# Two gated linear-attention blocks on one core: B's q by seven products per pair of row blocks, woven with B's k chunks

## The chip, the core and the metric

One core of one Trainium2 chip. The metric is the device time of one execution in microseconds; a kernel's time is the median of its runs. TensorE multiplies into PSUM (eight banks of 512 fp32 columns in each of 128 partitions), VectorE (DVE), ScalarE (ACT) and GpSimd (POOL) do the elementwise work, and SyncE (SP) issues most transfers.

## The reference

The input x has 2048 rows of 640 numbers. Two blocks, A and B, have weights of their own and read the same x. All data are bf16.

```python
def block(x, wqkv, wo):                       # A and B alike
    qkv = (x @ wqkv).reshape(B, S, 3, H, Dh)  # S = 2048, H = 32 heads of Dh = 20
    q, k, v = ...                             # each B, H, S, Dh
    phi = lambda t: jnp.where(t > 0, t + 1, jnp.exp(t)) + 1e-6
    pq, pk = phi(q), phi(k)
    kv  = einsum("bhsd,bhse->bhde", pk, v)
    z   = einsum("bhsd->bhd", pk)
    num = einsum("bhqd,bhde->bhqe", pq, kv)
    den = einsum("bhqd,bhd->bhq", pq, z)[..., None] + 1e-6
    return merge_heads(num / den) @ wo

g = sigmoid((x * gate_w).sum(-1, keepdims=True))
out = g * block(x, A_wqkv, A_wo) + (1 - g) * block(x, B_wqkv, B_wo)
```

## The kernel before

Rows are cut into 16 tiles of 128 (`ST`), features into 5 tiles of 128 (`DT`). `xT` holds x transposed (features on partitions), `xn` holds x with rows on partitions, `pk` holds phi(k) with rows on partitions and `pqT[b]` phi(q) transposed. v is never formed: G = xᵀ·pk is multiplied by wv (`kvt_mm`), masked to the heads' diagonal blocks (`kvt_mask`, into `KVT`), and multiplied by wo into one 640 x 640 matrix `M[b]` (`m_unit`), so that the output is pq·M. The row normalisation and the gate go into pqT (`rec_pass`, `norm_spread`, `scale`). Weights' columns are taken with a step of 5 (`mixed`), and every sum over features and every row tile is a group of matmuls in PSUM.

The order of the work:

1. A's k in 16 chunks (`k_chunk`: ten 128x320 matmuls, L205), with half of A's q between them (`q_block`, `q_unit`: ten 128x512 matmuls, L265 and L254). `phi` follows each: ScalarE takes the exponential (L195), VectorE clamps it (L198) and takes the maximum with the value plus one from PSUM (L202). In the "lifted" form ScalarE also copies the value plus one to SBUF (L197), and VectorE's maximum is a bf16 TensorTensor (L200).
2. The rest of A's q (`q_pass(0, ...)`), with the gate (`gate_pass`) and z (`z_rows`, `z_pass`).
3. A's G (`g_all`): one plain column block (`g_pass`, L288), then `g_strassen`, which computes a 2 x 2 block product by seven products instead of eight (L315). Its bf16 sums are `x_sum` and `k_sum` on VectorE. In its middle stand `rec_pass` (denominators on TensorE, then two steps `d` and two reciprocals on VectorE) and `norm_spread` (exA, L491), which TensorE does between two of the seven products.
4. B's k in 16 chunks, with A's `kvt_pass` after the second and four `p_diff` (sums for the output stage) on VectorE.
5. B's q (`q_pass(1, ...)`): ten units, with z and A's five `m_unit` between them.
6. B's G, as A's.
7. B's M, then the output: eight `Pair`s of row tiles, again seven products for a 2 x 2 block product of [pqA pqB] and [M_A; M_B].

Most of the instruction order is written by hand (`manual_schedule`); each engine runs its queue in order. PSUM in stages 1 to 6 is one pool of four slots of two banks (`ps0` to `ps3`), taken in turn unless a slot is named. A buffer's next user waits for the last reader of the one before. B's weights reuse A's buffers: `wk[1]` is loaded when A's last k chunk is done, `wq[1]` when A's q is done, `wv[1]` behind A's `kvt_pass`, B's wo behind A's last `m_unit`. All four go out on SP's queue, in that order and ahead of the output's stores.

Of the kernel before, what the change touches and what calls it, by code (L numbers as in the profile page):

```python
# [8 lines left out]
P = 128  # L9
# [22 lines left out]
def kernel(  # L32
# [19 lines left out]
    banks = ctx.enter_context(ExitStack())  # L52
    psum = banks.enter_context(tc.tile_pool(name="psum", bufs=1, space=bass.MemoryType.PSUM))

    turn = [0]

    def ps_raw(name, slot=None):

        if slot is None:
            slot = turn[0]  # L60
            turn[0] = (slot + 1) % 4
        return psum.tile([P, 4 * HB], BF16, tag=f"ps{slot}", name=name)
# [18 lines left out]
    R = persist.tile([P, 2, 4, RB], BF16, name="R")  # L81
    ones = persist.tile([P, H], BF16, name="ones")
    gwr = persist.tile([P, DT, H], BF16, name="gwr")
    D3 = persist.tile([P, DT, SH], BF16, name="D3")
# [6 lines left out]
    S3 = persist.tile([P, 3, hc, ic], BF16, name="S3")  # L91
    SX = {k: S3[:, k - 1] for k in (1, 2, 3)}
# [3 lines left out]
    lift = persist.tile([P, 1], FP32, name="lift")  # L96
    TM = [persist.tile([P, DT, HF], BF16, name="TM0")] + [None] * 3
    ge = [persist.tile([P, 2 * RB], FP32, name=f"ge{b}") for b in "AB"]
# [93 lines left out]
    def phi(dst, src, n, lifted=False):  # L192

        e = work.tile([P, 2, n], BF16, tag="e", name="e", bufs=3)
        nc.scalar.activation(out=e[:], in_=src, func=ACT.Exp)  # L195
        if lifted:
            nc.scalar.activation(out=dst, in_=src, func=ACT.Identity, bias=lift[:])  # L197
        nc.vector.tensor_scalar(e[:], e[:], 1.0, EPS, op0=ALU.min, op1=ALU.add)  # L198
        if lifted:
            nc.vector.tensor_tensor(out=dst, in0=dst, in1=e[:], op=ALU.max)  # L200
            return
        nc.vector.scalar_tensor_tensor(out=dst, in0=src, scalar=1.0 + EPS, in1=e[:], op0=ALU.add, op1=ALU.max)  # L202
# [7 lines left out]
    def k_done(b, i, pt):  # L210
        phi(pk[:, i, :].rearrange("p (b n) -> p b n", b=2), pt[:, :, 0:HF], HF)
# [32 lines left out]
    def mixed(t, m):  # L244

        return t[:, m::DT]

    def q_unit(b, m, h, lifted=False):

        pt = ps(f"q{'AB'[b]}")  # L250
        for u in range(2):
            for c in range(DT):
                n = 2 * h + u
                nc.tensor.matmul(  # L254
                    pt[:, u, :], lhsT=mixed(wq[b][:, c, :], m), rhs=xT[:, c, n * HB:(n + 1) * HB],
                    start=(c == 0), stop=(c == DT - 1),
                )
        phi(pqT[b][:, m, h * 2 * HB:(h + 1) * 2 * HB].rearrange("p (b n) -> p b n", b=2), pt, HB, lifted)

    def q_block(b, m, n):  # L260

        pt = ps(f"q{'AB'[b]}")
        for u in range(2):
            for c in range(DT):
                nc.tensor.matmul(  # L265
                    pt[:, u, :], lhsT=mixed(wq[b][:, c, :], m + u), rhs=xT[:, c, n * HB:(n + 1) * HB],
                    start=(c == 0), stop=(c == DT - 1),
                )
        phi(pqT[b][:, m:m + 2, n * HB:(n + 1) * HB], pt, HB)
# [94 lines left out]
    def z_rows(b):  # L364

        pt = ps(f"z{'AB'[b]}")
# [7 lines left out]
        zr = work.tile([P, D], BF16, tag="zr", name="zr")  # L374
# [6 lines left out]
    def z_pass(b, zr):  # L381

        pt = ps(f"zs{'AB'[b]}")
# [8 lines left out]
    def kvt_mm(b, pt, hf):  # L392

        for j in range(4):
            for c in range(DT):
                nc.tensor.matmul(  # L396
                    pt[:KG, hf, j * KG:(j + 1) * KG], lhsT=wv[b][:, c, (4 * hf + j) * KG:(4 * hf + j + 1) * KG],
                    rhs=GT[hf][:, c, j * KG:(j + 1) * KG], start=(c == 0), stop=(c == DT - 1),
                )

    def kvt_mask(pt, hf):

        nc.vector.tensor_tensor(
            out=KVT[:KG, 2 * hf:2 * hf + 2, 0:3:2, :],
            in0=pt[:KG, hf, 0:HF].rearrange("p (g k n) -> p g k n", g=2, k=2),
            in1=maskE[:KG, None, None, :].to_broadcast([KG, 2, 2, KG]), op=ALU.mult,
        )

    def kvt_pass(b):

        pt = ps("kvA")
        for hf in range(2):
            kvt_mm(b, pt, hf)
        for hf in range(2):
            kvt_mask(pt, hf)
# [106 lines left out]
    def tmp(name, tag):  # L522
        return work.tile([P, HF], FP32, tag=tag, name=name)

    class Pair:
# [13 lines left out]
        def p1(self):  # L539
            prod(self.at("x"), pqT[0][:, :, 0:SH], M[0][:, :, 0:HF], self.i, True)  # L540
            self.p1s = work.tile([P, HF], FP32, tag="e", name="p1s", bufs=3)
            nc.scalar.copy(out=self.p1s[:], in_=self.at("x"))
# [12 lines left out]
        def p6(self):  # L555
            prod(self.at("x"), xT[:, :, 0:SH], TM[1], self.i, False)
            self.u2 = tmp("u2", "ex")
            nc.scalar.copy(out=self.u2[:], in_=self.at("x"))  # L558
            self.u3 = tmp("u3", "zr")
            out_add(self.u3[:], self.at("y"), self.u2[:])  # L560
# [39 lines left out]
    def q_pass(b, units):  # L600

        units = list(units)
        q_unit(b, *units.pop(0))
        if b == 0:
            gate_pass()
        zr = z_rows(b)
        if b == 1:
            m_unit(0, 0, "act")
        for k in range(2):
            if b == 0:  # L610
                x_sum(1 + k)
            q_unit(b, *units.pop(0), b == 0)
        zsel = z_pass(b, zr)
        for k, (m, h) in enumerate(units):
            if b == 0 and k < 2:
                if k:
                    x_sum(3)
                else:
                    k_sum(0, 2)
            q_unit(b, m, h, b == 0)  # L620
            if b == 1 and k in (0, 2):
                for c in range(k + 1, k + 3):
                    m_unit(0, c, "act")
            if b == 1 and k == 0:
                k_sum(1, 1)
            if b == 1 and k == 4:
                add_rows(TM[0][:], M[0][:, :, HF:D], M[0][:, :, 0:HF], ALU.subtract)
        if b == 1:
            k_sum(1, 2)
        return zsel  # L630

    def g_all(b, zsel):

        g_pass(b, DT - 1, 1)
        k_sum(b, 3)
        g_strassen(b, zsel)

# [3 lines left out]
    turn[0] = 2  # L641
    for n in range(2):
        for i in range(CB if n else 0, CB * 2 * n):
            k_chunk(0, i)
        for m in (0, 2):
            q_block(0, m, n)
    q_unit(0, DT - 1, 0)
    for i in range(hc, ST - 2):
        k_chunk(0, i)
# [10 lines left out]
    def late_pool(name):  # L660
        return tc.tile_pool(name=name, bufs=1, space=bass.MemoryType.PSUM, reuse_waits="tile")

# [3 lines left out]
    with tc.manual_schedule():  # L666
# [5 lines left out]
        zsel = q_pass(0, [(m, 1) for m in range(DT)])  # L672
# [22 lines left out]
        part = [slice(n * RB, (n + 1) * RB) for n in range(4)]  # L695
# [3 lines left out]
        with late_pool("mid") as mid:  # L699
            first = bank(mid, "mid0", 2)  # L700
            kv = bank(mid, "mid1", 2)
            kvt_mm(1, kv, 0)
            kvt_mask(kv, 0)
            pairs[0].p1()
            kvt_mm(1, kv, 1)
            kvt_mask(kv, 1)
# [89 lines left out]
```

## Time and profile before

| | |
|---|---|
| median of 3 runs | 192.13 us (191.94 to 192.37) |
| the profiled execution | 192.89 us |
| its span, first to last instruction | 191.1 us, TensorE clock 1.000 |
| busy time | PE 185.4, DVE 146.9, ACT 74.0, POOL 8.5 us |
| A's k and first half of q | 7.8 to 41.6 us |
| A's q, rest, and A's G | 39.5 to 74.3 us |
| B's k | 74.3 to 97.5 us |
| B's q | 97.5 to 124.0 us |
| B's G | 124.0 to 145.3 us |
| B's M and the output | 145.3 to 191.1 us |

Times on the page are microseconds from the start of the span unless marked ns. A group's line gives the line of the code, the engine, the operation, output and inputs with their shapes, the count, then busy time and mean ns of one, then the idle time of the engine ahead of them and what ended it. In a timeline the first number is the start and the second the duration; an engine's sign with q (SPq) means its instruction queue, here a transfer's issue. Matmuls overlap: the pace of a run of matmuls is read from their starts. A few matmul records are missing from the trace.

### The profile page before, as it was taken

To read this page: it belongs to the slowest core of one execution; us is meant where nothing else is said; L and a number is where in the kernel's file an instruction comes from. 1 tells how busy PE (TensorE), PEld (TensorE's weight loads), DVE (VectorE), ACT (ScalarE), POOL (GpSimd) and SP (SyncE) were. 2 spreads that over 40 slices of the span, in tenths; PEclk is the share of its full clock that TensorE was granted. 3 is DMA by queue.
4 is the path that set the end of the run, shared out by engine and by line. 5 is a ranking of instruction groups with operands and counts; after the bars stand their busy time and mean duration, and the time that the engine had idled before them with its cause. 6 is when DMAs were issued, how large, how long until landed. Compare 5 with 4: busy or idle time off the path is not lost.

```text
span 191.1 us, 3763 instructions
## 1 busy us (share of the span) xinstructions
PE 185.4 (97%) x1567; PEld 125.1 (65%) x1575; DVE 146.9 (77%) x236; ACT 74.0 (39%) x104; POOL 8.5 (4%) x23
## 2 busy tenths in 40 slices
PE   8799999999999999999999999999999999999993
PEld 3466657765577677877765555577677776777772
DVE  1378968899893997799985785895797989788554
ACT  2055446455942532254544545431621611111120
POOL 8900000000000000000000000000000000000000
PEclk9999999999999999999999999999999999999999
DMA  6976549981050000320000006100000002312222
GB/s 175 328 142 86 106 77 368 301 198 50 2 172 3 0 0 0 67 108 0 3 0 0 3 2 144 31 0 0 3 0 0 3 0 70 125 70 71 74 77 69
DMA packets 18879, 13.99 MB, mean 73 GB/s; under 512 B 9392, under 2 KB 18864, under 8 KB 18864
## 3 DMA queue, kind: packets, MB, share of 16 engines
q1 hardware_dynamic: 18288, 13.11, 26.0%
q10 hardware_dynamic: 576, 0.66, 1.0%
q8 instruction: 12, 0.20, 0.5%
q14 instruction: 3, 0.02, 0.0%
HBM read 9.18 MB, written 2.62 MB: 62 GB/s over the span
## 4 chain that ended last, share of the span: by engine, by line
PE 93%; DMA 3%; DVE 1%; ACTq 0%; issue 0%; ACT 0%; DVEq 0%
PE gs L315 16%; PE qB L254 11%; PE kB L205 11%; PE kA L205 11%; PE qA L254 7%; PE ox L515 6%; PE oy L515 5%; PE oz L515 5%; PE qA L265 4%; DMA xn<-in_A_x_dram 3%; PE ow L515 2%; PE gB L288 2%; PE gA L288 2%; PE mA L429 2%; DVE osb L520 1%; PE mid L396 1%
## 5 line engine op out<-in xcount | busy, mean ns | idle before, releaser
L205 PEld LDWEIGHTS <-xT 128*128 128x128 bf16 x320 | 31.0, 98 | 12.5 <-DVE xT L190 0.5
L198 DVE TENSOR_SCALAR e<-e 128x640 bf16<-128x640 bf16 (+1 forms) x52 | 18.8, 361 | 11.6 <-ACT e L195 11.1
L205 PE MATMUL kA<-wkA,xT 128*128 128x320 bf16 x160 | 22.6, 299 | 0.1
L254 PE MATMUL qB<-xT,wqB 128*128 128x512 bf16 x96 | 22.3, 380 | 0.2
L205 PE MATMUL kB<-wkB,xT 128*128 128x320 bf16 x160 | 22.1, 299 | 0.0
L254 PEld LDWEIGHTS <-wqB 128*128 128x128 bf16 x100 | 11.4, 118 | 9.7 <-issue 0.7
L195 ACT ACTIVATE e<-kB 128x640 bf16<-128x640 f32 x16 | 11.3, 704 | 14.2 <-PE kB L205 12.2
L195 ACT ACTIVATE e<-kA 128x640 bf16<-128x640 f32 x16 | 11.1, 704 | 13.8 <-PE kA L205 13.8
L195 ACT ACTIVATE e<-qB 128x1024 bf16<-128x1024 f32 x10 | 10.2, 1023 | 12.7 <-PE qB L254 12.7
L202 DVE SCALAR_TENSOR_TENSOR pk<-kA,e 128x640 bf16<-128x640 f32 x16 | 13.2, 825 | 1.7
L202 DVE SCALAR_TENSOR_TENSOR pk<-kB,e 128x640 bf16<-128x640 f32 x16 | 13.2, 825 | 1.7
L195 ACT ACTIVATE e<-qA 128x1024 bf16<-128x1024 f32 x10 | 10.2, 1023 | 10.6 <-PE qA L254 5.2
L254 PE MATMUL qA<-xT,wqA 128*128 128x512 bf16 x58 | 13.5, 380 | 0.1
L202 DVE SCALAR_TENSOR_TENSOR pqTB<-qB,e 128x1024 bf16<-128x1024 f32 x10 | 12.3, 1225 | 1.4 <-DVE e L198 0.5
L558 ACT COPY u<-ox 128x320 f32<-128x320 f32 x8 | 3.4, 425 | 21.9 <-PE ox L515 21.9
L315 PEld LDWEIGHTS <-S 128*128 128x128 bf16 x96 | 9.1, 98 | 4.2 <-issue 0.8
L315 PEld LDWEIGHTS <-xn 128*128 128x128 bf16 x96 | 9.4, 98 | 3.6
L254 PEld LDWEIGHTS <-wqA 128*128 128x128 bf16 x60 | 6.9, 118 | 5.6 <-issue 0.3
L515 PEld LDWEIGHTS <-xT 128*128 128x128 bf16 x85 | 8.0, 98 | 3.1 <-DVE xT L454 0.2
L515 PEld LDWEIGHTS <-pqTA 128*128 128x128 bf16 x85 | 7.9, 98 | 2.9 <-issue 0.2
L515 PEld LDWEIGHTS <-pqTB 128*128 128x128 bf16 x80 | 7.8, 98 | 3.0
L315 PE MATMUL gs<-pk,xn 128*128 128x320 bf16 x64 | 9.3, 299 | 0.0
(121 smaller groups left out, 280.4 us busy)
## 6 DMA issues: line engine op xcount, KB each, us to landing
out_dram<-osb SPq DMA_DIRECT2D x14, 160.0 KB, 1.8
xn<-in_A_x_dram SPq DMA_DIRECT2D x3, 640.0 KB, 6.2
wqA<-in_A_wqkv_dram SPq DMA_DIRECT2D x1, 800.0 KB, 6.4
wvA<-in_A_wqkv_dram SPq DMA_DIRECT2D x1, 800.0 KB, 9.9
woA<-in_A_wo_dram SPq DMA_DIRECT2D x1, 800.0 KB, 11.9
wkB<-in_B_wqkv_dram SPq DMA_DIRECT2D x1, 800.0 KB, 4.7
wqB<-in_B_wqkv_dram SPq DMA_DIRECT2D x1, 800.0 KB, 4.6
wvB<-in_B_wqkv_dram SPq DMA_DIRECT2D x1, 800.0 KB, 4.7
```

The lines of the kernel that those rows point to most:

```text
L195: nc.scalar.activation(out=e[:], in_=src, func=ACT.Exp)
L198: nc.vector.tensor_scalar(e[:], e[:], 1.0, EPS, op0=ALU.min, op1=ALU.add)
L202: nc.vector.scalar_tensor_tensor(out=dst, in0=src, scalar=1.0 + EPS, in1=e[:], op0=ALU.add, op1=ALU.max)
L205: nc.tensor.matmul(pt[:, hf, 0:HF], lhsT=xT[:, c, i * P:(i + 1) * P], rhs=wk[b][:, c, hf * HF:(hf + 1) * HF], start=(c == 0), stop=(c == D ...
L254: nc.tensor.matmul(pt[:, u, :], lhsT=mixed(wq[b][:, c, :], m), rhs=xT[:, c, n * HB:(n + 1) * HB], start=(c == 0), stop=(c == DT - 1),)
L265: nc.tensor.matmul(pt[:, u, :], lhsT=mixed(wq[b][:, c, :], m + u), rhs=xT[:, c, n * HB:(n + 1) * HB], start=(c == 0), stop=(c == DT - 1),)
L288: nc.tensor.matmul(pt[:, hf, 0:HF], lhsT=xn[:, i, c * P:(c + 1) * P], rhs=pk[:, i, hf * HF:(hf + 1) * HF], start=(i == 0), stop=(i == ST - 1),
L315: nc.tensor.matmul(pt[:, n, 0:HF], lhsT=left[:, i, n * P:(n + 1) * P], rhs=right[:, i, :], start=(first and i == 0), stop=(i == hc - 1), s ...
L396: nc.tensor.matmul(pt[:KG, hf, j * KG:(j + 1) * KG], lhsT=wv[b][:, c, (4 * hf + j) * KG:(4 * hf + j + 1) * KG], rhs=GT[hf][:, c, j * KG:(j ...
L429: nc.tensor.matmul(dst[32 * g:32 * g + 32, :], lhsT=mixed(heads, c), rhs=wo_sb[b][:KG, 2 * g + k, hf * HF:(hf + 1) * HF], start=(k == 0), ...
L515: nc.tensor.matmul(dst, lhsT=left[:, c, r0:r0 + P], rhs=right[:, c, :], start=(first and c == 0), stop=(c == DT - 1), skip_group_check=not ...
L558: nc.scalar.copy(out=self.u2[:], in_=self.at("x"))
```

## The change

- **Seven products.** For B, the features 0 to 511 of x (two by two tiles), four of the five column tiles of wq and each pair of 512-row blocks form a 2 x 2 block product. `q_strassen` computes it with seven products of two matmuls each instead of eight; the fifth feature tile is added plainly, and the fifth column tile stays plain (`fifth`). Sums of products are made in the PSUM banks: ScalarE seeds one bank with a copy of another, VectorE adds a saved product (`p5`) from one bank into two others.
- **The sums it needs.** `sq_sum` makes four sums of x for each pair of row blocks, on VectorE: for rows 0 to 1023 between the clamp and the top of three q phis of A and behind one k chunk, for rows 1024 to 2047 ahead of A's `g_strassen`. `tq_sums` makes four sums of wqB on POOL, as soon as wqB has landed.
- **The weave.** B's k chunks 0 to 2 and half of the fifth column tile come first, then four calls of `q_strassen`; in each, up to four fillers (B's k chunks 3 to 15, A's `kvt` as `Masks`, the other half of the fifth column tile) stand between the products. PSUM in this stage is four single banks (`quad`) for the products and two two-bank slots for the fillers.
- **phi** is split into its ScalarE part (when `Phi` is made), `clamp` and `top`, so that other VectorE work can stand between. Three q phis of A become lifted.
- **What moves.** `p_diff`, A's `m_unit`s, B's z, B's first two `k_sum`s and the `TM0` sum now stand behind the weave; B's wv and wo are loaded behind their buffers' new last readers. `D3` shares its buffer with the sums of x, one of the G stage's sums of x is made in place in `xn`, the output's `u2` and `u3` take the buffers of `d1` and `e`, and PSUM's banks are handed out in stages.

The diff, cut to its core:

```diff
-    SX = {k: S3[:, k - 1] for k in (1, 2, 3)}
+    SX = {k: S3[:, k - 1] for k in (1, 2)}
+    SX[3] = xn[:, 0:hc, ic:2 * ic]
...
+    def phi(dst, src, lifted=False, between=None):
+        f = Phi(dst, src, lifted)
+        f.clamp()
+        if between is not None:
+            between()
+        f.top()
...
+    def sq_sum(k, r):
+        lo, hi = [slice(n * HB, (n + 1) * HB) for n in (2 * r, 2 * r + 1)]
+        x11, x12, x21, x22 = [xT[:, c:c + 2, rows] for rows in (lo, hi) for c in (0, 2)]
+        a, b, op = {
+            1: (x21, x22, ALU.add), 2: (SQ[:, 0, r], x11, ALU.subtract),
+            3: (x11, x21, ALU.subtract), 4: (x12, SQ[:, 1, r], ALU.subtract),
+        }[k]
+        nc.vector.tensor_tensor(out=SQ[:, k - 1, r], in0=a, in1=b, op=op)
+
+    def tq_sums(b):
+        w = [[wq[b][:, c:c + 2, :].rearrange("p c (f t) -> p c t f", t=DT)[:, :, m:m + 2] for m in (0, 2)] for c in (0, 2)]
+        (w11, w12), (w21, w22) = w
+        for k, x, y in ((0, w12, w11), (1, w22, TQ[0]), (2, w22, w12), (3, w21, TQ[1])):
+            nc.gpsimd.tensor_tensor(out=TQ[k], in0=x, in1=y, op=ALU.subtract)
+
+    def q_strassen(b, m, r, quad, fills):
+        ce, cf, co, cz = quad
...
+        prod(ce, w_of(m), x_of(lo), (0, 1), True)
+        nc.scalar.copy(out=co, in_=ce)
+        a = work_of()
+        a.clamp()
+        a.top()
+        prod(cz, tq(1), sq(1), (0, 1), True)
+        p5 = work.tile([P, HB], FP32, tag="osb", name="p5", bufs=3)
+        nc.scalar.copy(out=p5[:], in_=cz)
+        prod(co, tq(2), sq(2), (0, 1), False)
+        add(cf, co, p5[:])
+        prod(ce, w_of(m), x_of(lo), (2, 3, 4), False)
+        f = Phi(pqT[b][:, m, rows(lo)], ce)
+        f.clamp()
+        f.top()
+        a = work_of()
+        a.clamp()
+        prod(co, tq(3), sq(3), (0, 1), False)
+        add(cz, co, p5[:])
+        a.top()
+        prod(cf, lambda c: natural(c + 2 * (c < 2), m + 2), lambda c: sq(4)(c) if c < 2 else x_of(lo)(c), (0, 1, 4), False)
+        f = Phi(pqT[b][:, m + 2, rows(lo)], cf)
+        f.clamp()
+        f.top()
+        a = work_of()
+        a.clamp()
+        a.top()
+        prod(co, lambda c: tq(4)(c) if c < 2 else natural(c, m), lambda c: x_of(hi)(c + 2 * (c < 2)), (0, 1, 4), False)
+        prod(cz, w_of(m + 2), x_of(hi), (4,), False)
+        f = Phi(pqT[b][:, m:m + 3:2, rows(hi)], [co, cz], True)
+        a = work_of()
+        f.clamp()
+        f.top()
+        if a is not None:
+            a.clamp()
+            a.top()
...
+            for m in (0, 2):
+                q_block(0, m, n, (lambda k: lambda: sq_sum(k, 0))(1 + m // 2) if n else None)
+        q_unit(0, DT - 1, 0, True, None, lambda: sq_sum(3, 0))
+        for i in range(hc, ST - 2):
             k_chunk(0, i)
+            if i == hc:
+                sq_sum(4, 0)
...
         wq[1] = load_w(1, "q", nc.sync)
-        g_all(0, zsel)
-        turn[0] = 3
-        for i in range(ST):
-            k_chunk(1, i)
-            if i == 1:
-                kvt_pass(0)
-                wv[1] = load_w(1, "v", nc.sync)
-            if i in (3, 6, 9, 12):
-                r0 = (i - 3) // 3 * RB
-                p_diff(slice(r0, r0 + RB))
+        g_pass(0, DT - 1, 1)
+        k_sum(0, 3)
+        for k in range(1, 5):
+            sq_sum(k, 1)
+        g_strassen(0, zsel)
+        tq_sums(1)
+        new_stage("weave")
+        k_chunk(1, 0, 3)
+        k_chunk(1, 1, 2)
+        quad = [cell(f"q{n}", n)[:] for n in range(4)]
...
+        f = fifth(0, quad[1:3])
+        f.clamp()
+        f.top()
+        k_chunk(1, 2, 3)
+        fills = [chunk(3, 2), lambda: Masks(3)]
+        fills += [chunk(i, 2 + i % 2) for i in range(4, ST)]
+        fills.insert(13, lambda: fifth_two(1, 3))
+        fills[14:] = [chunk(ST - 1, 2), lambda: None]
+        for m, r in ((0, 0), (1, 0), (0, 1), (1, 1)):
+            q_strassen(1, m, r, quad, fills[:4])
+            fills = fills[4:]
...
-        zsel = q_pass(1, [(m, h) for h in range(2) for m in range(DT)])
+        k_sum(1, 1)
+        k_sum(1, 2)
         load_wo(1, nc.sync)
-        g_all(1, zsel)
-        banks.close()
+        new_stage("after")
+        g_pass(1, DT - 1, 0)
+        zr = z_rows(1, 1)
+        part = [slice(n * RB, (n + 1) * RB) for n in range(4)]
+        for rows in part:
+            p_diff(rows)
+        for c in range(DT):
+            m_unit(0, c, "act", ps("mA", (2, 3, 1)[c % 3]))
+        zsel = z_pass(1, zr, 2)
+        k_sum(1, 3)
+        add_rows(TM[0][:], M[0][:, :, HF:D], M[0][:, :, 0:HF], ALU.subtract)
+        g_strassen(1, zsel)
+        new_stage(None)
```

More of the change, by code (lines that the diff above doesn't have):

```diff
@@ L246, in mixed, with q_mm, q_two @@
         return t[:, m::DT]
-    def q_unit(b, m, h, lifted=False):
-        pt = ps(f"q{'AB'[b]}")
-        for u in range(2):
-            for c in range(DT):
-                n = 2 * h + u
+    def q_mm(b, m, n, c, dst, first, last):
+        nc.tensor.matmul(
+            dst, lhsT=mixed(wq[b][:, c, :], m), rhs=xT[:, c, n * HB:(n + 1) * HB],
+            start=first, stop=last,
+        )
+    def q_two(b, parts, pt):
+        for u, (m, n) in enumerate(parts):
+            for c in range(DT):
+                q_mm(b, m, n, c, pt[:, u, :], c == 0, c == DT - 1)
@@ new lines, in tq_sums, with natural, x_of, prod @@
+    def tq_sums(b):
[5 more added lines that the diff above has]
+        ce, cf, co, cz = quad
+        lo, hi = 2 * r, 2 * r + 1
+        fill = iter(fills)
+        def natural(c, t):
+            return mixed(wq[b][:, c, :], t)
+        def x_of(n):
+            return lambda c: xT[:, c, n * HB:(n + 1) * HB]
+        def prod(dst, left, right, cs, first):
+            for k, c in enumerate(cs):
@@ L254, in q_unit @@
                 nc.tensor.matmul(
-                    pt[:, u, :], lhsT=mixed(wq[b][:, c, :], m), rhs=xT[:, c, n * HB:(n + 1) * HB],
-                    start=(c == 0), stop=(c == DT - 1),
-                )
[L258 to L269, printed above, removed]
+                    dst, lhsT=left(c), rhs=right(c), start=first and k == 0, stop=k == len(cs) - 1,
@@ new lines, in prod, with w_of, tq, sq @@
+                    skip_group_check=not first,
+                )
+        def w_of(t):
+            return lambda c: natural(c, t)
+        def tq(k):
+            return lambda c: TQ[k - 1][:, c, m, :]
+        def sq(k):
+            return lambda c: SQ[:, k - 1, r, c, :]
+        def rows(n):
+            return slice(n * HB, (n + 1) * HB)
+        def add(dst, src, sb):
+            nc.vector.tensor_tensor(out=dst, in0=src, in1=sb, op=ALU.add)
+        def work_of():
+            return next(fill)()
@@ L379, in z_rows, with z_pass @@
         return zr
-    def z_pass(b, zr):
-        pt = ps(f"zs{'AB'[b]}")
+    def z_pass(b, zr, slot=None):
+        pt = ps(f"zs{'AB'[b]}", slot)
         for c in range(DT):
@@ new lines, in fifth_two, with chunk, go, __init__ @@
+        def fifth_two(h, slot):
+            pt = ps("qB", slot)
+            return fifth(h, [pt[:, 0], pt[:, 1]])
+        def chunk(i, slot):
+            def go():
+                pt = ps("kB", slot)
+                for hf in range(2):
+                    for c in range(DT):
+                        k_mm(1, i, c, pt, hf)
+                return Phi(pk[:, i, :].rearrange("p (b n) -> p b n", b=2), pt[:, :, 0:HF])
+            return go
+        class Masks:
+            def __init__(self, slot):
+                self.pt = ps("kvA", slot)
+                for hf in range(2):
+                    kvt_mm(0, self.pt, hf, hf)
+                wv[1] = load_w(1, "v", nc.sync)
+            def clamp(self):
+                kvt_mask(self.pt, 0, 0)
+            def top(self):
+                kvt_mask(self.pt, 1, 1)
```

162 lines of the change are left out of this document (87 added, 75 removed).

## The prediction

> **What bounds the kernel now.** First the page: the shares of the engines and the chain of work that ended last.
>
> ```profile
> PE 185.4 (97%) x1567; PEld 125.1 (65%) x1575; DVE 146.9 (77%) x236; ACT 74.0 (39%) x104; POOL 8.5 (4%) x23
> ...
> PE 93%; DMA 3%; DVE 1%; ACTq 0%; issue 0%; ACT 0%; DVEq 0%
> ```
>
> The chain is TensorE almost from end to end: from 7.3 us, when x has landed, to 185.2 us there is no gap of note. Only fewer matmuls shorten it, and only while the other engines keep up. How full VectorE is, stage by stage, comes from the windows (busy us of PE, PEld, DVE, ACT, POOL):
>
> ```profile
> 50.00:60.00 10.00, 10.00 (x86) 6.67 (x88) 7.46 (x11) 5.76 (x8) 0.00 (x0) 1.00 0.26 83
> ...
> 80.00:90.00 10.00, 10.00 (x76) 7.22 (x74) 8.53 (x16) 5.42 (x8) 0.00 (x0) 1.00 0.22 77
> ...
> 110.00:120.00 10.00, 9.95 (x72) 5.59 (x73) 7.10 (x8) 5.04 (x7) 0.00 (x0) 1.00 0.36 81
> ```
>
> B's k chunks (80 to 90) leave VectorE little room, B's q (110 to 120) some 3 us in 10. Then the timelines of B's q, of B's k and of A's G stage:
>
> ```profile
> 115.13 8.83 PE L254 MATMUL qB<-xT,wqB 128*128 128x512 bf16 x39
> ...
> 123.80 4.51 PE L288 MATMUL gB<-pk,xn 128*128 128x320 bf16 x32
> ...
> 83.90 0.32 DVE L198 TENSOR_SCALAR e<-e 128x640 bf16<-128x640 bf16 x1
> ...
> 84.33 0.82 DVE L202 SCALAR_TENSOR_TENSOR pk<-kB,e 128x640 bf16<-128x640 f32 x1
> ...
> 85.07 0.32 DVE L198 TENSOR_SCALAR e<-e 128x640 bf16<-128x640 bf16 x1
> ...
> 52.98 0.37 SPq L593 DMA_DIRECT2D wqB<-in_B_wqkv_dram  x1
> ...
> 56.29 1.48 DVE L454 TENSOR_TENSOR pqTB<-pk 128x2560 bf16<-128x2560 bf16 x1
> ...
> 60.73 0.42 DVE L444 SCALAR_TENSOR_TENSOR d<-denA,geA 128x256 f32<-128x256 f32 x1 [2.96 <-PE denA L169]
> ...
> 63.25 1.75 DVE L449 RECIPROCAL rT<-d 128x256 bf16<-128x256 f32 x1
> ...
> 65.06 0.40 PE L491 MATMUL exA<-rT,spread 32*128 32x256 bf16 x8
> ```
>
> Three readings. A 512-wide matmul costs (123.80 - 115.13)/40 = 0.217 us (one of the 40 has no record). A k chunk occupies VectorE 1.17 us (83.90 to 85.07): a dependent instruction starts 0.10 after the end of the one before, an independent one 0.08 before it. And VectorE idles 2.96 us before 60.73, but then every step to exA is tight: the reciprocals end at 65.00, and TensorE comes to exA at 65.06. The durations:
>
> ```profile
> L200 DVE TENSOR_TENSOR pqTA<-pqTA,e 128x1024 bf16<-128x1024 bf16 x4 | 2.8, 693 | 0.9 <-ACT pqTA L197 0.6
> ...
> L202 DVE SCALAR_TENSOR_TENSOR pqTB<-qB,e 128x1024 bf16<-128x1024 f32 x10 | 12.3, 1225 | 1.4 <-DVE e L198 0.5
> ...
> L180 ACT ACTIVATE geA<-lg 128x512 f32<-128x512 f32 x1 | 0.6, 597 | 0.2 <-PE lg L169 0.2
> ...
> L153 POOL TENSOR_SCALAR_AFFINE_SELECT E<-E 32x640 bf16<-32x640 bf16 x8 | 5.7, 712 | 0.4
> ...
> L145 POOL TENSOR_SCALAR_AFFINE_SELECT maskE<-maskE 128x80 bf16<-128x80 bf16 x2 | 0.5, 270 | 0.1
> ```
>
> **The change, part by part.** *TensorE.* One call of q_strassen has 2+2+2+3+2+3+3+1 = 18 matmuls where four plain outputs need 20. Four calls save 8; the instruction order of the changed program has 1567 matmuls for 1575. 8 x 0.217 = **-1.73 us**. Three changes from q to a narrower group also go: 99.61 - 97.36 for ten matmuls is 0.08 over 2.17, the two ahead of mA are 0.10 over. Some return around Masks; I take **-0.15** of 0.28.
>
> *The weave* (from 74.3 us). TensorE needs 18 x 0.217 + 4 x 1.36 = 9.34 us a call with four k chunks. VectorE: chunks 4 x 1.17 = 4.68; two adds of 128x512 from PSUM (490 ns at 128x320 and 824 at 128x640, so 0.69), 0.61 each without the overlap, 1.22; two phis of 128x512 (clamp 0.29, top 0.69 by the slopes of L198 and L202) 1.00 each; the lifted pair 0.53 + 0.61. That is 9.04, or 8.87 because the add stands between a clamp and its top in the second filler: 95% of TensorE's time. ScalarE has eight 512-wide passes of 0.5 and four exponentials of 0.6 to 0.7, about 6.7. Shares are not enough, so I walked the queues of one call. T is the end of the cz product of the call before. ScalarE has its four passes and one exponential done and co copied by T+3.35; TensorE wants co at T+3.58. VectorE frees the bank of the call's first chunk at T+1.5; it is wanted at T+1.79. The second add has read co by T+8.0; wanted at T+8.46. Slacks of 0.2 to 0.5, and VectorE waits some 0.35 at the lifted pair in each call: **0**, and VectorE could even enter the weave 2.5 us late. If that cover is gone, each of its 16 instructions a call costs directly (second rival).
>
> *Sums of x, rows 0 to 1023.* Three q tops become a ScalarE pass plus a two-input TensorTensor (1225 to 693 ns) and make room for sq_sum 1 to 3; the fourth stands behind a k chunk. By the walk from 24.4 us VectorE is 0.57 late at 32.6 and gains 1.36 - 1.17 = 0.19 a chunk, so it is level again before the last. Four PSUM slots cover that: **0**.
>
> *Sums of x, rows 1024 to 2047.* Four TensorTensors of 693 ns behind k_sum(0, 3): 57.69, 58.48 (dependent), 59.09, 59.71 to 60.40. They fill the idle 2.96 us, 0.33 before d may start at 60.73: **0**, if they run at 693 ns. What comes later than 60.73 is paid in full at exA, where d and two reciprocals stand in the same queue.
>
> *Sums of wqB on POOL.* They wait for wqB: issued at 52.98, 4.6 us to land, so 57.6, just as those sums start. Their readers come at about 82, so POOL's own length is hidden. The trace has no POOL sum. From the selects, (712 - 270)/560 = 0.79 ns an element, 512 elements in one pass are 0.61 us; two inputs at most twice that, 1.2. What VectorE suffers beside them is between 0 and four whole instructions. No gain is possible, as nothing is taken away there. I take 0: the only rows with both engines busy (the xT copies from 4.6 to 9.7 us, 289 ns for 256 elements and 348 for 384) lie near one line with the 492 ns for 640, of which POOL covers only the first 0.2 us; but those have one input in PSUM, which is why the other end stays as a rival.
>
> [...]
>
> *B behind the weave.* W is its end, VectorE is free at W+2.9. gB ends at W+4.35, zB at W+5.45. VectorE does two k_sums (1.48 each) to W+5.9, zr to W+6.7, four p_diffs to W+9.6, zsel, k_sum 3, TM0 to W+12.2; denB ends at W+12.4, so d is not late. TensorE waits twice: the third m_unit takes zB's slot and waits for zr, 0.11; z_pass takes the slot of the fourth m_unit and waits for ScalarE's copy, 0.2. **+0.3.**
>
> *SP's queue.* wvB goes out behind Masks, near 85 us for 78.5, woB behind A's last m_unit, near 126 for 115; they land 4.7 and 5.8 us later, first used beyond 143: 0. u2, u3 and p1s keep two buffers each: 0. The output stage is the same.
>
> Sum: -1.73 - 0.15 + 0.3 = -1.58. The profiled execution took 192.89 us (span 191.1 and 1.79 around it) and would become 191.3; the median of the runs is 192.13, 0.76 lower, so the forecast on that scale is **190.5 us**.
>
> **Rivals.** (a) *POOL blocks VectorE's sums.* POOL's first sum and the four sq_sums begin within 0.2 us of each other. If the two engines take turns, all four POOL sums come before the last sq_sum: 4 x 0.61 to 4 x 1.2 = 2.4 to 4.9 late, less the slack of 0.4: +2.0 to +4.5, or 192.5 to 195.0, slower. It decides from 1.9 us of blocking. For: the coincidence and the tight chain to exA. Against: k_sum and the sq_sums stand back to back, with 0.1 us of gap at the dependent one, so POOL may only get in at 60.4, when VectorE turns to d and reciprocals. If one POOL sum slips in, 0.2 to 0.8 is lost, which stays inside the forecast. [...]
> (b) *VectorE bounds the weave.* Its margin is 9.34 - 8.87 = 0.47 a call, 0.03 us an instruction. If adds into PSUM or half-width phis run 0.05 longer, some 0.6 us go over the calls; at 0.08, 2.0: 191.1 to 192.5. For: no row has a 128x512 form on VectorE. Against: all are between measured sizes.
> (c) *That the products aren't saved* is excluded by the instruction order.
>
> **The numbers.** Forecast 0.58: own range 190.2 to 191.3. (a) 0.27, all slower. (b) 0.12: 0.05 faster, 0.04 no change, 0.03 slower. Something unseen 0.03, put to no change. A measurement here can tell 0.2%, 0.38 us. So faster 0.63, same 0.07, slower 0.30. The range reaches from 190.1 to the middle of (a), 193.8, and leaves out about 0.14 above and 0.03 below.
>
> **What would show it.** Right: 1567 matmuls less the unrecorded; q calls 9.3 us apart; exA starting right behind x12's product; sq_sums at 0.69; two waits of 0.1 to 0.2 ahead of the third mA and zsB. Wrong: a TensorE gap ahead of exA with sq_sums longer than 0.7 or apart (a); TensorE waits on VectorE's adds or tops inside the weave (b); POOL sums of many us.

## The result, and the profile after

The changed kernel takes **194.81 us** (median of 9 runs, 192.78 to 195.26) against 192.13 us before (9 runs, 191.84 to 192.44): the ratio is 1.0121, interval 1.0085 to 1.0157. It is slower by 2.7 us, where 190.5 was forecast. Seven of the nine runs have a mean granted TensorE clock of 0.991 and a time of 194.6 or more; the other two have 1.000, and they are the two shortest (192.78 and 192.92). The profiled execution is one of the seven: 195.26 us, span 193.6 (before: 192.89 and 191.1).

The page of the changed kernel: the engines' shares, the granted clock in 40 slices of the span, and the shares in the chain that ended last.

```profile
PE 186.3 (96%) x1558; PEld 125.3 (65%) x1567; DVE 156.4 (81%) x262; ACT 86.2 (45%) x133; POOL 15.2 (8%) x27
...
PEclk9999999999999969999999999999999999999999
...
PE 73%; DVE 17%; DMA 5%; ACT 2%; issue 1%; ACTq 0%; DVEq 0%
```

Two things are new. VectorE has 17% of the chain, where it had 1%: somewhere TensorE has become the engine that waits. And one slice in the row of the clock shows a 6; before, all 40 are at 9. TensorE is busy 0.9 us more, with 9 matmuls fewer on record. The slice with the 6 is at 68 to 73 us, in A's G stage. The timeline of the changed kernel there:

```profile
57.40 0.68 DVE L324 TENSOR_TENSOR SQ<-xT 128x1024 bf16<-128x1024 bf16 x1
57.58 1.41 POOL L331 TENSOR_TENSOR TM<-wqB 128x512 bf16<-128x512 bf16 x1 [47.89 <-DMA wqB<-in_B_wqkv_dram]
58.12 1.41 DVE L324 TENSOR_TENSOR SQ<-SQ,xT 128x1024 bf16<-128x1024 bf16 x1
59.06 1.58 POOL L331 TENSOR_TENSOR TM<-wqB,TM 128x512 bf16<-128x512 bf16 x1
...
59.46 1.74 DVE L324 TENSOR_TENSOR SQ<-xT 128x1024 bf16<-128x1024 bf16 x1
...
60.60 2.06 POOL L331 TENSOR_TENSOR MB<-wqB 128x512 bf16<-128x512 bf16 x1
...
61.12 2.09 DVE L324 TENSOR_TENSOR SQ<-xT,SQ 128x1024 bf16<-128x1024 bf16 x1
...
62.62 1.72 POOL L331 TENSOR_TENSOR MB<-wqB,TM 128x512 bf16<-128x512 bf16 x1
...
63.13 0.41 DVE L571 SCALAR_TENSOR_TENSOR d<-denA,geA 128x256 f32<-128x256 f32 x1
...
65.76 0.29 PE L618 MATMUL exA<-rT,spread 32*128 32x256 bf16 x4 [0.91 <-DVE d L571]
...
67.45 0.29 PE L618 MATMUL exA<-rT,spread 32*128 32x256 bf16 x4 [1.41 <-DVE rT L576]
67.68 4.02 PE L450 MATMUL gs<-pqTB,xn 128*128 128x320 bf16 x16
...
71.53 2.34 PE L450 MATMUL gs<-pqTB,S 128*128 128x320 bf16 x16
```

Read it from the top. The first sum of x (SQ) takes 0.68 us. GpSimd's first sum of wqB (TM; the later two go to MB) starts 0.18 us behind it. From there on every sum of either engine is long: VectorE's next three take 1.41, 1.74 and 2.09 us, GpSimd's four 1.41, 1.58, 2.06 and 1.72. Start plus duration gives the ends: 58.08 (VectorE), 58.99 (GpSimd), 59.53, 60.64, 61.20, 62.66, 63.21, 64.34. They alternate strictly: VectorE always ends 0.55 behind GpSimd, GpSimd 0.9 to 1.5 behind VectorE, and so the long durations hold a wait for the other engine's instruction. In this same trace the four sums of x for rows 0 to 1023 take 0.68 to 0.69 us each (25.5 to 32.9 us, GpSimd idle). Beside that, 0.72 to 1.40 us of VectorE's later three are wait; of GpSimd's four it is only 0.31 to 0.46, by their lengths alone (1.04, 1.27, 1.60 and 1.28 us, measured below). Each of these ends falls one such length, less 0.13 to 0.16 us, behind the end before it: on these sums the two engines work one after the other. VectorE's last sum ends at 63.21 and d starts at 63.13 (an independent instruction starts 0.08 early). In the kernels in which d waits for TensorE (the one before, and GpSimd later, below), it starts 0.12 behind the start of the G product beside it (60.73 and 60.61 before, 60.31 and 60.19 in GpSimd later). That product starts at 60.32 here, so d could have started at 60.44 and is 2.7 us late. Both halves of exA, which before ran as one piece without a wait, now come late. TensorE finished x12's product at 65.76 - 0.91 = 64.85, and begins the next G product at 67.68.

The second loss stands in the last two lines: the 16 matmuls from 67.68 need 3.85 us to the next product, and the later ones need 2.18 (71.53 to the next at 73.71). The windows of the changed kernel say why (the last three numbers are the granted clock, the DMA share and the GB/s):

```profile
67.50:67.75 0.25, 0.25 (x5) 0.13 (x5) 0.25 (x1) 0.00 (x0) 0.00 (x0) 1.00 0.00 0
67.75:68.00 0.25, 0.25 (x3) 0.17 (x4) 0.25 (x1) 0.23 (x1) 0.00 (x0) 0.93 0.00 0
68.00:68.25 0.25, 0.25 (x3) 0.14 (x2) 0.25 (x1) 0.25 (x1) 0.00 (x0) 0.50 0.00 0
...
71.25:71.50 0.25, 0.25 (x3) 0.14 (x2) 0.25 (x1) 0.00 (x0) 0.00 (x0) 0.74 0.00 0
71.50:71.75 0.25, 0.25 (x4) 0.18 (x2) 0.25 (x1) 0.01 (x1) 0.00 (x0) 1.00 0.00 0
```

A quarter of a microsecond at 0.93 is full clock for 0.86 of it, so the clock halves at 67.96; by the 0.74 it is back at 71.38. For 3.4 us TensorE runs at half speed, just when it has work again.

The balance of the profiled execution, counted from the first transposes behind the load of x (7.35 us before, 7.07 after) to the first k chunk of B: +4.24. From x12's product to the next one 2.83 us pass instead of the 0.33 of exA in one piece, so 2.50 of it is standstill; 3.85 - 2.18 = 1.67 is the half clock; that is 4.17 of the 4.24. From B's first k chunk to B's first G product the kernel gains 54.05 - 52.60 = 1.45, and everything behind that takes as long as before (62.79 and 62.78). With the 0.28 by which it starts earlier, +4.24 - 1.45 - 0.28 = 2.5 us, which is the difference of the spans.

### The profile page after: what moved, and what is told of

Same layout as the page of the kernel before. It is cut to its first block, busy times and chain, and to the rows that moved or that the text cites. A ratio compares the mean times of both kernels' runs of the same rounds, so it can differ in the third digit from the quotient of the medians.

```text
span 193.6 us, 3814 instructions
## 1 busy us (share of the span) xinstructions
PE 186.3 (96%) x1558; PEld 125.3 (65%) x1567; DVE 156.4 (81%) x262; ACT 86.2 (45%) x133; POOL 15.2 (8%) x27
## 4 chain that ended last, share of the span: by engine, by line
PE 73%; DVE 17%; DMA 5%; ACT 2%; issue 1%; ACTq 0%; DVEq 0%
PE gs L450 13%; PE kA L249 11%; PE kB L249 11%; PE q L347 7%; PE ox L642 6%; PE qA L293 6%; PE oy L642 5%; PE oz L642 5%; DVE SQ L324 3%; DMA xn<-in_A_x_dram 3%; PE ow L642 2%; DMA wkB<-in_B_wqkv_dram 2%; DVE rT L576 2%; DVE pqTB L581 1%; DVE S L581 1%
## 5 line engine op out<-in xcount | busy, mean ns | idle before, releaser
L229 DVE TENSOR_SCALAR e<-e 128x640 bf16<-128x640 bf16 (+2 forms) x56 | 19.3, 345 | 8.9 <-ACT e L224 8.6
L249 PE MATMUL kB<-wkB,xT 128*128 128x320 bf16 x160 | 24.2, 299 | 0.0
L249 PE MATMUL kA<-wkA,xT 128*128 128x320 bf16 x160 | 23.3, 305 | 0.0
L293 PE MATMUL qA<-xT,wqA 128*128 128x512 bf16 x96 | 22.2, 379 | 0.2
L293 PEld LDWEIGHTS <-wqA 128*128 128x128 bf16 x100 | 11.6, 118 | 9.3 <-issue 0.3
L450 PEld LDWEIGHTS <-xn 128*128 128x128 bf16 x128 | 13.0, 103 | 5.9 <-issue 0.2
L224 ACT ACTIVATE e<-qA 128x1024 bf16<-128x1024 f32 x10 | 10.2, 1023 | 8.6 <-PE qA L293 8.1
L224 ACT ACTIVATE e<-q 128x512 bf16<-128x512 f32 x18 | 10.8, 597 | 5.0 <-PE q L347 3.4
L347 PE MATMUL q<-xT,wqB 128*128 128x512 bf16 x32 | 9.5, 379 | 0.0
L647 DVE TENSOR_TENSOR osb<-oz,u 128x320 bf16<-128x320 f32 (+1 forms) x18 | 8.0, 451 | 1.6 <-PE oz L642 0.9
L423 PEld LDWEIGHTS <-xn 128*128 128x128 bf16 x64 | 6.3, 98 | 3.0 <-issue 0.4
L669 ACT COPY p1s<-ox 128x320 f32<-128x320 f32 x8 | 3.4, 425 | 10.3 <-PE ox L642 10.3
```

Of the source, the lines that this page charges most:

```text
L224: nc.scalar.activation(out=to, in_=part, func=ACT.Exp)
L229: nc.vector.tensor_scalar(self.e, self.e, 1.0, EPS, op0=ALU.min, op1=ALU.add)
L249: nc.tensor.matmul(pt[:, hf, 0:HF], lhsT=xT[:, c, i * P:(i + 1) * P], rhs=wk[b][:, c, hf * HF:(hf + 1) * HF], start=(c == 0), stop=(c == D ...
L293: nc.tensor.matmul(dst, lhsT=mixed(wq[b][:, c, :], m), rhs=xT[:, c, n * HB:(n + 1) * HB], start=first, stop=last,)
L347: nc.tensor.matmul(dst, lhsT=left(c), rhs=right(c), start=first and k == 0, stop=k == len(cs) - 1, skip_group_check=not first,)
L423: nc.tensor.matmul(pt[:, hf, 0:HF], lhsT=xn[:, i, c * P:(c + 1) * P], rhs=pk[:, i, hf * HF:(hf + 1) * HF], start=(i == 0), stop=(i == ST - 1),
```

## The experiments

The theory after the result: the sums of wqB on GpSimd and the sums of x on VectorE hold each other up, d comes 2.7 us late, TensorE stands at exA, and behind the standstill its clock is halved for one stretch. The rivals: the sums of x alone are too much for VectorE there; the weave itself loses; or the fall of the clock has its own cause (GpSimd, both engines at work at once, the more TensorE work before) and only happens beside the wait. Each kernel was timed in five rounds beside the kernel before.

**GpSimd later.** One column of the last sum of x is copied by GpSimd ahead of its sums, so that they start behind VectorE's.

```diff
+    gate = persist.tile([P, 1], BF16, name="gate")
...
+        nc.gpsimd.tensor_copy(out=gate[:], in_=SQ[:, 3, 1, 1, 0:1])
         tq_sums(1)
```

> One POOL instruction (a copy of one column of the last sum of x) stands ahead of the four sums of wqB, so that POOL starts them only when VectorE's four sq_sums are through; nothing else differs from the changed kernel. Theory 1 (the loss is made in A's G: POOL's and VectorE's two-input sums take turns, d is 2.8 us late, TensorE stands 2.4 us ahead of exA and then runs some 4 us at half clock): sq_sums back at 0.69, no gap ahead of exA, clock 1.000, 190.6 us (190.3 to 191.2). Theory 2 (the rest of the change costs too, the sums are only part of it): the gap goes but the time stays at 191.5 or above. If POOL blocks k_sum 4 and the scales instead, up to 1 us more than theory 1.

Measured: **190.78 us** (190.26 to 191.02), ratio 0.9917, interval 0.9891 to 0.9943; granted clock 1.00. The timeline of this kernel at the same place:

```profile
59.20 0.68 DVE L325 TENSOR_TENSOR SQ<-xT,SQ 128x1024 bf16<-128x1024 bf16 x1
60.02 0.19 POOL L787 COPY gate<-SQ 128x1 bf16<-128x1 bf16 x1 [50.30 <-DVE SQ L325]
60.16 1.04 POOL L332 TENSOR_TENSOR TM<-wqB 128x512 bf16<-128x512 bf16 x1
...
60.31 0.42 DVE L572 SCALAR_TENSOR_TENSOR d<-denA,geA 128x256 f32<-128x256 f32 x1 [0.43 <-PE denA L193]
...
64.06 1.28 POOL L332 TENSOR_TENSOR MB<-wqB,TM 128x512 bf16<-128x512 bf16 x1
64.50 2.19 DVE L582 TENSOR_TENSOR pqTB<-pk,pqTB 128x2560 bf16<-128x2560 bf16 x1
...
64.64 0.40 PE L619 MATMUL exA<-rT,spread 32*128 32x256 bf16 x8
```

VectorE's sums take 0.68 again, d even waits 0.43 us for TensorE, as the prediction had it for four sums at 693 ns, and exA is one piece without a gap. All the sums are still made; only their order in time differs. So the sums of x are not too much for VectorE, and the weave does not lose. TensorE's work ahead of exA is the same, too, and the clock stays up (1.00 in every 2 us from 38 to 76 us). GpSimd's first two sums, beside d and the reciprocals, take 1.04 and 1.25 us, and these instructions of VectorE are not lengthened (0.42 and 1.75). At the end the two engines meet once more: a k_sum of 1.43 us starts 0.44 into GpSimd's last sum and takes 2.19. Nobody waits for it.

**GpSimd's sums left out.** The kernel does not make the sums of wqB; its products use wqB's own columns in their place.

```diff
-            return lambda c: TQ[k - 1][:, c, m, :]
+            return lambda c: natural(c, m)
...
-        tq_sums(1)
```

> The sums of wqB are left out: the products that used them take wqB's own columns, so the same matmuls run on other weights. Theory 1: POOL idle after 10 us, sq_sums at 0.69, 190.5 us, within 0.3 of the gated kernel; what the gated kernel has over this one is what POOL still costs. Theory 2: 191.5 or above.

Measured: 190.60 us (190.28 to 191.09), ratio 0.9914, interval 0.9888 to 0.9940. No different from GpSimd later: once out of VectorE's way, the four sums cost nothing that these runs can tell.

**GpSimd's sums in the kernel before.** The same four instructions are added to the kernel before at the same place, written to a buffer that is not in use yet.

```diff
...
+        tq_sums(1)
         g_all(0, zsel)
```

> The kernel before with only the four POOL sums of wqB added at the same point, into a buffer that is not used yet; no sum of x on VectorE beside them. Theory 1: there is no two-input VectorE instruction between 57.8 and 64.9 us for them to take turns with, so d and the reciprocals are on time: 192.1, no change within 0.2%; POOL's sums take 1.0 to 1.4 us each. Rival (POOL's work itself slows VectorE, TensorE or the chain to exA): 192.6 or more.

Measured: 192.14 us (191.67 to 192.97) against 192.15, ratio 1.0002, interval 0.9982 to 1.0022. GpSimd's sums in this kernel:

```profile
57.85 1.04 POOL L370 TENSOR_TENSOR D<-wqB 128x512 bf16<-128x512 bf16 x1 [48.16 <-DMA wqB<-in_B_wqkv_dram]
58.96 1.27 POOL L370 TENSOR_TENSOR D<-wqB,D 128x512 bf16<-128x512 bf16 x1
...
60.19 1.60 POOL L370 TENSOR_TENSOR D<-wqB 128x512 bf16<-128x512 bf16 x1
...
61.75 1.28 POOL L370 TENSOR_TENSOR D<-wqB,D 128x512 bf16<-128x512 bf16 x1
```

They run beside VectorE's idle time, d and the reciprocals. So these are their lengths alone. Neither engine's work by itself costs time here (GpSimd's sums alone: ratio 1.0002; VectorE's alone, in the kernel above: 190.60 us); the pair does (194.81).

**VectorE's sums later.** The four sums of x are moved behind A's G stage, to the start of the weave.

```diff
-        for k in range(1, 5):
-            sq_sum(k, 1)
         g_strassen(0, zsel)
+        for k in range(1, 5):
+            sq_sum(k, 1)
```

> The changed kernel with the four sums of x for rows 1024 to 2047 behind A's g_strassen instead of ahead of it; POOL's sums stay where they are. Theory 1: POOL's sums (57.6 to about 63 us) meet no two-input VectorE instruction and take 1.0 to 1.6 us each, exA has no gap, the clock stays at 1.000; VectorE enters the weave 2.6 us late, which the walk of the prediction says the weave covers but for some 0.1: 190.6 to 190.9. If that cover was overrated, each us that VectorE is late shows as TensorE waits on VectorE's tops in the weave: 191.5 to 193.

Measured: 190.74 us (190.41 to 191.60), ratio 0.9926, interval 0.9900 to 0.9952. GpSimd takes 1.04, 1.26, 1.61 and 1.27, as alone, and exA has no gap. The weave swallows 2.6 us more of VectorE's work at its start without a loss (from B's first k chunk to B's first G product it takes 52.6 us, as in the changed kernel), which the prediction had claimed ("VectorE could even enter the weave 2.5 us late").

**The sums of wqB on VectorE.** They are made behind A's G instead, with `nc.vector` for `nc.gpsimd`.

> The changed kernel with the four sums of wqB on VectorE, where they stand in the program behind A's g_strassen, and nothing on POOL. Theory 1: sq_sums at 0.69, exA without a gap, clock 1.000. The new cost is four VectorE sums with a stepped input at the start of the weave, 0.5 to 0.7 us each, 2 to 2.8 in all, within the cover of 2.5: 190.5 to 190.9. If the cover was overrated: 191.5 to 193.

Measured: 190.96 us (190.43 to 191.31), ratio 0.9931, interval 0.9907 to 0.9955. wqB's columns are read with a step of five elements; the 512 elements take 0.73 to 0.74 us on VectorE, 0.57 of GpSimd's mean, and lie in the same slack.

These five settle the first half: each of the orders tried that keeps the two engines' sums apart lies about 4 us below the changed kernel. The next ones are on the clock.

**Dummy matmuls in the standstill.** Ahead of exA, TensorE gets 11 matmuls of 512 columns whose results nobody reads; sums and wait stay as they are.

```diff
+        if b == 0:
+            hold = ps("hold", 3)
+            for k in range(11):
+                nc.tensor.matmul(hold[:, 0, :], lhsT=xn[:, k, 4 * P:5 * P], rhs=pk[:, k, 0:HB], start=True, stop=True)
         norm_spread(b, rts, (2, 3))
```

> The changed kernel with eleven 512-wide matmuls (11 x 0.217 = 2.4 us of added work, results unused) ahead of exA, where TensorE otherwise stands still. Theory 1: the wait stays as long (sq_sums still 1.4 to 2.1 us) but TensorE is busy through it, so the clock stays at 1.000 and the time is 192.8 to 193.0, some 1.9 us below the changed kernel although it does more. Rival (the half clock has another cause than the standstill): clock 0.99 and 194.8 or more.

Measured: 192.95 us (192.53 to 194.40, 12 runs), ratio 1.0046, interval 1.0020 to 1.0072. The timeline of this kernel:

```profile
60.46 2.09 DVE L324 TENSOR_TENSOR SQ<-xT,SQ 128x1024 bf16<-128x1024 bf16 x1
...
63.99 2.54 PE L484 MATMUL hold<-pk,xn 128*128 128x512 bf16 x10
...
66.46 0.62 PE L622 MATMUL exA<-rT,spread 32*128 32x256 bf16 x8
...
67.02 2.35 PE L450 MATMUL gs<-pqTB,xn 128*128 128x320 bf16 x16
```

VectorE's sums are as long as in the changed kernel (2.09 for the last), so exA is as late, but the dummies (2.54 us; one of the 11 has no record) keep TensorE busy, the clock stays at 1.00 (in every 2 us from 38 to 76 us), and the G product behind takes 2.35 instead of 4.02. Useless work makes the kernel faster: the median is 1.9 us lower, the ratio to the kernel before 1.0046 instead of 1.0121. It also agrees with the two runs of the changed kernel with a clock of 1.000 (192.78 and 192.92): the standstill alone is worth that time. Three of the 12 runs lie at 194.0 to 194.4 with a clock of 1.00; what they lost is not shown.

With only **five dummies** (`range(5)`):

> As the kernel that holds the clock, with five added matmuls instead of eleven, so that 1.1 of the 2.4 us are filled and some 1.3 us of standstill stay. Theory 1: same wait, so 192.9 where the clock holds and 194.6 where it falls to half for some 4 us; a standstill of this length tells where the clock begins to fall. If 1.3 us are too short for it: 192.9 and clock 1.000 in nearly all runs; if not: 194.6, as the changed kernel.

Measured: 193.54 us (193.23 to 193.92, 6 runs), ratio 1.0069, interval 1.0046 to 1.0093; clock 0.998 to 1.000. The dummies cover the first half of the standstill; ahead of exA's second half TensorE still stands 1.23 us:

```profile
67.13 0.29 PE L622 MATMUL exA<-rT,spread 32*128 32x256 bf16 x4 [1.23 <-DVE rT L580]
...
67.35 2.35 PE L450 MATMUL gs<-pqTB,xn 128*128 128x320 bf16 x16
```

No half clock follows (1.00 in each microsecond from 64 to 72 us), and the next G product takes 2.35. One gap of 1.23 us was not enough for a fall in any of the six runs. The profiled execution (193.29 us) is 0.35 longer than that with 11 dummies (192.94), and this lies ahead of the first transposes behind the load of x (6.72 against 6.38 us): from there to B's first k chunk both take 69.34 us. So the dummies that were left out are no loss there; why the medians differ by 0.6 us is not shown.

**Lateness without GpSimd.** So far every kernel with a fallen clock had both engines' sums. Here GpSimd's are left out as above, and VectorE makes its sums nine times instead of four.

```diff
-        for k in range(1, 5):
+        for k in (1, 1, 1, 2, 2, 3, 3, 4, 4):
             sq_sum(k, 1)
```

> GpSimd has no sums of wqB here (the products use wqB's own columns), and VectorE makes its sums of x for the rows 1024 to 2047 nine times in place of four, ahead of A's G: five sums more, of 0.61 to 0.72 us each, some 3.2 us, less the 0.42 us that d waited for TensorE: d is 2.8 us late, as in the changed kernel, with no GpSimd instruction beside. Theory (lateness of d alone makes both losses): TensorE stands 2.3 to 2.7 us ahead of exA, and the granted clock falls to 0.50 for some 3.7 us behind that; 190.6 of the kernel without the sums of wqB + 2.4 + 1.7 = 194.7 us, granted clock 0.991. Rival (the fall of the clock belongs to GpSimd's instructions, or to both engines drawing on SBUF at once): the standstill alone, 193.0 us, and the clock stays at 1.00.

Measured: **195.55 us** (194.79 to 196.08), ratio 1.0162, interval 1.0136 to 1.0188. Every run but the profiled one has a clock of 0.991, and that one has 0.982. Timeline and windows of the profiled one:

```profile
61.32 1.41 DVE L324 TENSOR_TENSOR SQ<-xT,SQ 128x1024 bf16<-128x1024 bf16 x2
...
65.28 0.29 PE L618 MATMUL exA<-rT,spread 32*128 32x256 bf16 x4 [1.35 <-DVE d L571]
...
66.97 0.40 PE L618 MATMUL exA<-rT,spread 32*128 32x256 bf16 x4 [1.40 <-DVE rT L576]
```

```profile
66.25:66.50 0.25, 0.00 (x0) 0.00 (x0) 0.25 (x1) 0.00 (x0) 0.00 (x0) 0.56 0.00 0
...
73.00:73.25 0.25, 0.25 (x3) 0.12 (x2) 0.00 (x0) 0.00 (x0) 0.00 (x0) 0.79 0.00 0
```

The sums are short (0.7 each), there is no GpSimd, and yet both losses are back: 1.35 + 1.40 of waits, then half a clock. The theory expected 194.7; the rival that puts the fall down to GpSimd, 193.0. So neither GpSimd's sums nor both engines' at once are needed for the fall: the clock is at 0.50 in each microsecond from 67 to 73 us without them. The theory is 0.85 low, mostly since TensorE stands longer than the 2.4 us that it took: x12's product ends at 65.28 - 1.35 = 63.93, and the next G product starts at 67.30, 3.04 us behind it when exA's 0.33 is taken off. In this execution the clock is at half from 66.28 to 73.11 by the same reckoning, 6.8 us, twice as long as in the changed kernel. That gives its clock of 0.982, and it is the longest of the six runs.

**Less late.** The same with `(1, 1, 2, 2, 3, 4)`, two extra sums.

> As the run with five extra sums, but with two extra, some 1.3 us less 0.42: d is 0.9 us late. Theory (a short standstill does not move the clock): TensorE stands 0.6 to 0.9 us ahead of exA, granted clock 1.00, 190.6 + 0.8 = 191.4 us. Rival (any standstill here costs the clock as well): 193.1 us, with a stretch at 0.50.

Measured: 191.46 us (190.79 to 192.74, 12 runs), ratio 0.9966, interval 0.9945 to 0.9986; clock 1.00. d starts at 61.41, 0.94 us late. TensorE stands once, for 0.65 us ahead of exA's second half:

```profile
65.74 0.29 PE L618 MATMUL exA<-rT,spread 32*128 32x256 bf16 x4 [0.65 <-DVE rT L576]
```

The whole cost is 191.46 - 190.60 = 0.86 us: this short standstill does not move the clock (1.00 in each microsecond from 64 to 69 us). The border that these kernels show lies between one gap of 1.23 us, which does not, and a pair of 0.91 and 1.41, which mostly does.

**The waits behind the weave.** The prediction gave 0.3 us to two small TensorE waits behind the weave. This kernel has GpSimd later as above, moves one k_sum behind z_rows, and gives z_pass slot 1 in place of 2. It changes part of the computation: in one G product a part of the seed is not added (read from the code, not from a trace). The same matmuls run.

```diff
         k_sum(1, 1)
-        k_sum(1, 2)
...
         zr = z_rows(1, 1)
+        k_sum(1, 2)
...
-        zsel = z_pass(1, zr, 2)
+        zsel = z_pass(1, zr, 1)
```

> The gated kernel with two more edits behind the weave: zr stands ahead of B's second k_sum on VectorE, and z_pass takes the slot of the third m_unit instead of the fourth's. Theory: the two TensorE waits there (0.4 us together in the gated kernel) go, 0.4 us below the gated kernel: 190.4. If they were covered by something else that comes next (d and the reciprocals of B), no gain: 190.8.

Measured: 191.51 us (190.53 to 192.03, 12 runs), ratio 0.9970, interval 0.9949 to 0.9990. It gains nothing over GpSimd later alone (190.78), and is rather slower. The timeline shows the two waits gone and two others in their place:

```profile
121.80 2.94 PE L557 MATMUL mA<-woA,KVT 80*32 80x320 bf16 x80
...
124.68 0.37 PE L521 MATMUL zsB<-I,zr 128*128 128x32 bf16 x5
...
127.48 1.28 PE L193 MATMUL denB<-pqTB,zsel 128*32 128x256 bf16 x40 [0.25 <-DVE zsel L525]
...
133.96 0.29 PE L619 MATMUL exB<-rT,spread 32*128 32x256 bf16 x4 [0.54 <-DVE rT L577]
```

zsB now follows mA at once (2.88 us after its start). But VectorE has its k_sum later in the queue, so zsel and the reciprocals come late: 0.25 ahead of denB and 0.54 ahead of exB. From B's first k chunk to B's first G product it gains 0.56 us on GpSimd later (52.05 against 52.61), and from there to the end it loses 1.1 (64.0 against 62.9), 0.79 of it in these two waits. Here a wait for VectorE does not vanish when TensorE is allowed to come earlier; it is met further on. The profiled execution, 190.53 us, is short because x came early in it: from the first transposes behind the load to the end it takes 182.8 us (188.9 - 6.12), GpSimd later 182.3 (189.2 - 6.94). Why the other runs spread up to 192.0 is not shown.

The best version is the one with GpSimd later: 190.78 us, 0.8% below the kernel before and some 2% below the changed one.

## Why the prediction was wrong

**What failed.** The step "Sums of wqB on POOL ... I take 0", and with it the condition in "Sums of x, rows 1024 to 2047": "0, if they run at 693 ns". Three of the four ran at 1.41, 1.74 and 2.09. Rival (a), at 0.27, is what happened, by its own mechanism: the engines take turns, three of GpSimd's four sums go before the last sum of x (it had counted four), and d is 2.7 us late behind its slack, inside its +2.0 to +4.5. That 194.81 us, too, lies inside its 192.5 to 195.0 is luck: (a) had only the standstill, which is worth 192.85, and the rest is the clock.

The bad argument was the one against (a): that GpSimd would find only 0.1 us of room between back-to-back sums and "may only get in at 60.4". A gap is not needed. VectorE's third sum starts at 59.46, 0.07 before the second ends, and is still held up: GpSimd's second, on record from 59.06, ends first, at 60.64, and VectorE's third at 61.20. The evidence taken against blocking, the xT copies at the start, has one operand in PSUM; in the runs, too, d and the reciprocals (one operand from PSUM, or one in all) run beside GpSimd unharmed: 0.42 and 1.75 us with GpSimd later, as before. So those rows could not speak for instructions with two operands in SBUF, and the prediction itself said so. The range for GpSimd's length, 0.61 to 1.2 us, was low for three of the four: alone they take 1.04, 1.27, 1.60 and 1.28. In these traces, of two such sums on both engines at once, the one that started second was the long one: GpSimd's 1.04 became 1.41, VectorE's 0.69 became 2.09, and a k_sum of 1.43 became 2.19. With neither of the two reasons against it holding, (a) deserved more than 0.27.

**What was not foreseen at all.** The fall of the clock, 1.67 us in the profile and 194.81 - 192.85 = 2.0 us between the runs with and without it. No term and no rival held it. Without it the result would have been the 192.85 of those two runs, near the lower end of (a). Rival (a) priced the standstill at its own length; here a standstill in two parts, 0.91 and 1.41 us, cost a stretch of half speed as well.

**What was right.** The other terms can be read from the runs in which the sums are apart, at 190.6 to 191.0 against a forecast of 190.5:
- Matmuls and transitions, -1.73 - 0.15, and the two waits, +0.3, are -1.58 from B's first k chunk to B's G; measured -1.45. Two errors nearly cancel in it. From the first of mA to zsB the changed kernel takes 3.49 us, the kernel without the two waits 2.88, so the waits cost 0.61 and not 0.3. With -1.73 for the matmuls, -0.33 is then left for the transitions, more than the -0.15 taken (before, the same 80 matmuls stood in three places and took 0.65 + 1.30 + 1.23 = 3.18).
- The weave at 0: the four calls of q_strassen start at 84.45, 93.94, 103.26 and 112.58 in the changed kernel, 9.32 apart (9.49 with the Masks), where 9.34 was worked out. VectorE's new forms take 690 ns (adds of 128x512) and 691 (tops), as interpolated (0.69). Rival (b) did not occur.
- Sums of x, rows 0 to 1023, at 0: in the run with GpSimd later, the time from the first transposes behind the load of x to B's first k chunk is 66.90 us, before 66.91.
- SP's queue and the output stage at 0: from B's first G product to the end, 62.79 us before and 62.78 after.

## What to carry to other kernels

When work is moved to GpSimd, look which VectorE instructions with two operands in SBUF run at the same time, and put GpSimd behind them by a dependency: here such sums of VectorE went from 0.69 to as much as 2.09 us beside GpSimd's, one copied column was worth 4 us, and the sums themselves were free. A wait of TensorE is priced with the half clock that can follow it: single gaps of 0.65 and 1.23 us left the clock alone, a pair of 0.9 and 1.4 cost 1.7 to 2.0 us more in seven runs of nine. What VectorE may do "in idle time" ahead of a tight chain is safe only at the durations it has beside what else runs there (four sums at 0.69 fitted here, at up to 2.09 they made d 2.7 us late).

## What was not expected of the hardware

- The turns are strict in these traces. While both engines had such sums to do, one instruction of each went in turn, and the time recorded for an instruction includes its wait for the other: VectorE's 0.69 becomes 1.41 to 2.09, growing with GpSimd's own length (1.04 to 1.60).
- GpSimd's length for 512 elements depends on more than their number: 1.04, 1.27, 1.60 and 1.28 in the kernel before, and within 0.02 of that in two others. The first and the third both read wqB twice with a step of five elements, so that step alone does not decide it; what does was not tried.
- Only two traces show both ends of the half clock: 67.96 to 71.38 is 3.42 us in the changed kernel, 66.28 to 73.11 is 6.83, twice that, in the one with nine sums of x. A mean clock of 0.991, as in the other runs that have the fall, is what one stretch of 3.42 gives (half of 3.42 is 0.009 of 193 us). In the changed kernel it begins when TensorE is working again (from 67.68), in the other during the second wait (65.57 to 66.97). Two gaps of 0.91 and 1.41 us, 0.29 us of work between them, were enough in seven runs of nine; why two runs keep the full clock is not shown. Whether the sum of the gaps counts was not tried by itself.
